# A fused attention and feed-forward kernel: the first batch loaded and ordered anew

## The chip, the core and the metric

The kernel runs on one core of a Trainium2 chip. The core has a matrix engine (TensorE, PE in the profile, with its weight loads listed apart as PEld), a vector engine (VectorE, DVE), a scalar engine (ScalarE, ACT), a general engine (GpSimd, POOL) and a queue engine (SyncE, SP) that only issues transfers. All transfers run on 16 DMA engines. Matrix products are written to PSUM, where this kernel holds eight banks of 2 KB per partition. The metric is the device time of one execution in microseconds, as the median of several runs.

## The reference, cut to what matters

```python
def _attn_ref(q, k, v):                     # (8, 12, 448, 64) each, float32
    scores = (1.0 / np.sqrt(64)) * np.matmul(q, k.transpose(0, 1, 3, 2))
    attn = np.maximum(scores, 0.0) ** 2 / 448
    return np.matmul(attn, v)

x = attn_out.transpose(0, 2, 1, 3).reshape(3584, 768)   # batch*seq, heads*dim
h = x @ w_in                                # w_in (768, 2048)
r = np.maximum(h, 0.0)
out = (r * r) @ w_out                       # w_out (2048, 768)
```

There is no softmax: the scores are cut at zero, squared and multiplied by v. So keys can be added up in any order, and every step after the scores is elementwise or a product.

## The kernel before

**Units and rounds.** The twelve heads of a batch are taken four at a time; such a group is a unit, three to a batch and 24 in all. A unit's 448 keys are cut into seven sets of 64; one set of one unit is a round. For a round the kernel computes scores (L348: 64x64 products, four of them side by side in the array), cuts them at zero out of PSUM into the buffer `rel` (L374 on DVE or L377 on ACT), squares them into `at` or `comb` (L381 on ACT or L383 on POOL) and multiplies by v (L411, again 64x64 products). The result of a unit leaves PSUM as part of `xt` (L431 or L433), the transposed x.

**Getting q and k into shape.** `load_qk` (L241) loads q or k of a unit as float32 (448 KB), `cast_qk` (L266) makes float16 of it in one of three buffers `blk` (L271), and `turn_pe` (L281) turns it: seven 128x128 transposes on PE (L288) into a bank of PSUM and one copy to `qkt` (L291) by DVE or ACT. Later units are turned by a DMA instead. For the first batch, the loads of unit 0 go to buffers `raw`, those of units 1 and 2 into a buffer `early`, which is one of the two large `g` buffers read as float32. The casts of units 1 and 2 are given to POOL alone, that of unit 0 to DVE or ACT. `load_v` (L309) loads v of a unit by two POOL DMAs (L317) that cast to float16 on the way; the quarters of w_in (`load_w1`, L322) and w_out (`load_w2`, L327) are POOL DMAs that cast as well.

**The feed-forward part.** `h_pair` (L488, first batch) and `h_group` (later batches) multiply `xt` with w_in (L472); h is squared by ACT out of PSUM (L461), masked by DVE (L456), and lands in `g`. Output products are L561 for a part of the first batch and L623 later, where a seven-product scheme for 2x2 blocks is used, with sums made by DVE (L602) and of the weights by POOL (L587). Results leave by L545, L547 and L635 and are stored by SP (L510).

**The order of the work.** Every step is added to a list (`Plan.add`) with the engines that may do it, a duration for each, what it depends on, and a due time. `Plan.run` (L71) then walks through a modelled time: whenever an engine is free in the model, `pick` (L152) hands it the waiting step with the earliest due time that is ready and finds free buffers, and the instruction is emitted there and then. The engines run their instructions in exactly this order, so a step that the model takes for late stands behind others even where its data come early. The engine's first free times are given in L230, and until the modelled time `plan.cold` (L231) PE costs are multiplied by 1.6. In the model, transfers pass one after the other at 390 GB/s. A step on PE that is bound to 64x64 products has the mode "tile", others "dense", and the model charges 0.09 or 0.235 us for a change (`SWITCH`).

**The first batch** is written by hand (L752 to L821). PE first runs twelve products on a zeroed buffer (L756). The 448 queries are cut in two parts, 256 and 192 columns. Two rounds make a tile; part 0 has the tiles 0 to 10 and part 1 the tiles 11 to 21 (tile 10 holds one round, as does 21). Tile after tile is scored, with the v products `put` two or three tiles later, and from tile 13 on one h product group of part 0 between (`first_h.popleft()`, L805). The turns of units 1 and 2 stand at tiles 1 to 4, those of unit 3 at tiles 17 and 19 (L778).

Two buffers of two banks each hold scores (`sp`), and four banks (`mm`) serve turns, v products, h and outputs.

Of the kernel before, what the change touches and what calls it, by code (L numbers as in the profile page):

```python
# [41 lines left out]
class Plan:  # L42
# [6 lines left out]
    def __init__(self, pools, busy):  # L49
        self.pools = {name: [(0.0, i, t) for i, t in enumerate(ts)] for name, ts in pools.items()}  # L50
        self.busy = busy
        self.ops: list = []
        self.now = 0.0
# [17 lines left out]
    def run(self):  # L71
# [20 lines left out]
        while done < n_ops:  # L92
# [6 lines left out]
            while again:  # L99
                again = False  # L100
                for eng in ("PE", "ACT", "DVE", "POOL", "SP"):
# [3 lines left out]
                    if got is None:  # L105
                        continue
# [16 lines left out]
                    if size:  # L123
                        dma = max(dma, begin + 1.2) + size / 390e3
                        op.end = dma + 1.0
                    if len(rest) > 1:
                        self.busy["POOL"] = max(self.busy["POOL"], self.busy[eng])
# [23 lines left out]

    def pick(self, eng, now, waiting):  # L152
        for z, (_, _, op) in enumerate(waiting):
            if op.ready > now + 1e-9:
                continue
            for alt in op.alts:
                if alt[0] != eng:
                    continue
                if len(alt) > 5 and self.busy["POOL"] > now + 0.4 and op.due > now:
                    continue  # L160
                need: dict = {}
                for b in op.bufs:
                    if b.tile is None:
                        need[b.pool] = need.get(b.pool, 0) + 1
                if all(sum(x[0] <= now + 1e-9 for x in self.pools[p]) >= k
                       for p, k in need.items()):
                    return z, alt
        return None
# [3 lines left out]
def kernel(  # L172
# [57 lines left out]
    plan = Plan(pools, {"PE": 5.8, "ACT": 2.6, "DVE": 1.2, "POOL": 1.4, "SP": 0.7})  # L230
    plan.cold = 32.0  # L231
# [9 lines left out]
    def load_qk(n, w, after=0.0, gate=False):  # L241
        b, u = divmod(n, NU)
        if n in (1, 2):
            buf, z = early, 2 * n - 2 + (w == "k")
        else:
            buf, z = Buf("raw"), None

        def tile_of():
            if z is None:
                return buf.tile  # L250
            return buf.tile[:, 4 * z:4 * z + 4].rearrange("p f s -> p (f s)").bitcast(
                FP32).rearrange("p (f x) -> p f x", f=2)
# [12 lines left out]

    def cast_qk(n, w, raw, names=("POOL",)):  # L266
# [10 lines left out]
        return plan.add([alts[x] for x in names], [load], [buf, blk]), blk  # L277
# [3 lines left out]
    def turn_pe(n, w, cast, at=None):  # L281
        op, blk = cast
        ps, to = Buf("mm"), Buf("qkt")

        def flip():
            flat = ps.tile.bitcast(FP16)
            for t in range(TJ):
                nc.tensor.transpose(flat[:, t * P:(t + 1) * P], blk.tile[:, t, :], ident)  # L288
# [11 lines left out]
    def turn_dma(n, w, cast):  # L300
        op, blk = cast
# [7 lines left out]
    def load_v(n, after=0.0):  # L309
# [9 lines left out]
        vst[n] = plan.add([("POOL", 1.25, 1.25, emit, QK)], bufs=[buf], after=after), buf  # L319

    def load_w1(i, after):
        return plan.add([("POOL", 0.85, 0.85, lambda: nc.gpsimd.dma_start(  # L322
            out=w1[i], in_=moe_w_in[:, 512 * i:512 * (i + 1)].rearrange(
                "(m p) f -> p m f", p=P)), WQ)], after=after)

    def load_w2(hf, i, after):
# [3 lines left out]
                "(f p) d -> p f d", p=P)), WQ)], after=after)  # L330
# [177 lines left out]
    def store(op, places, cols, osb):  # L508
        def emit(i, b, t):
            return lambda: nc.sync.dma_start(  # L510
# [3 lines left out]
        for i, (b, t) in enumerate(places):  # L514
            plan.add([("SP", 0.56, 3.0, emit(i, b, t))], [op], [osb], due=plan.now + 8.0)
# [167 lines left out]

    fifo: deque = deque()
# [72 lines left out]

    early = Buf("g")
    raws, casts = {}, {}
    for n in range(NU):  # L760
        for w in "kq":
            raws[n, w] = load_qk(n, w)
    for n in range(NU):
        for w in "kq":
            casts[n, w] = cast_qk(n, w, raws[n, w], ("POOL",) if n else ("DVE", "ACT"))
    for n, after in enumerate((1.4, 7.7, 10.0)):
        load_v(n, after)
    w1_ops = [load_w1(0, 12.0), load_w1(1, 13.5)]
    for w in "kq":
        raws[3, w] = load_qk(3, w, 14.5, True)  # L770
    w1_ops += [load_w1(2, 15.0), load_w1(3, 16.0)]
# [6 lines left out]
    turns = {1: (1, "k"), 2: (1, "q"), 3: (2, "k"), 4: (2, "q"), NA + 6: (3, "k"), NA + 8: (3, "q")}  # L778
# [3 lines left out]
    def put(i):  # L782
        part, rs = tiles[i]
        for n, t in rs:
            ats[n, t] = held.pop((part, n, t))
            av(n, [t], PARTS[part])

    for i, (part, rs) in enumerate(tiles):
# [3 lines left out]
        op = scores(rs, [sp], cols, True, 7.6 + 1.25 * i)  # L792
# [7 lines left out]
        if 2 <= i < NA + 2:  # L800
            put(i - 2)
        if i >= NA + 3:
            put(i - 3)
        if i > NA + 1:
            first_h.popleft()[1]()  # L805
        if i == NA:
            for w_ in "kq":
                casts[3, w_] = cast_qk(3, w_, raws[3, w_])
                raws[4, w_] = load_qk(4, w_, 24.0, True)
            load_v(3, 26.0)  # L810
            w2_ops = [[load_w2(hf, z, 29.0 + 6.0 * hf + z) for z in range(2)] for hf in range(2)]
            for w_ in "kq":
                raws[5, w_] = load_qk(5, w_, 35.0, True)
            load_v(4, 36.0)
# [3 lines left out]
    for i in range(len(tiles) - 3, len(tiles)):  # L818
        put(i)
        first_h.popleft()[1]()  # L820
# [37 lines left out]
    for j in sorted(j for j in pushes if j >= NB):  # L858
        push_dense(pushes[j])
    run_some(1e9)  # L860
# [31 lines left out]
```

## Time and profile before

| | us |
|---|---|
| median of 14 runs (lowest, highest) | 398.06 (396.26, 399.56) |
| the profiled execution | 397.69 |
| its span, first to last instruction | 395.9 |
| PE busy in the span | 377.5 (95%) |
| ACT / DVE / POOL busy | 268.6 / 264.6 / 222.8 |
| first score product | 12.41 |
| first h product | 29.04 |

Times within the profile count from the span's start. The line number behind an instruction names the line of the kernel before. In an answer in order of time, the columns are start, duration, engine, line, operation, written from read tile, shapes, count, and in square brackets how long the engine stood idle before it and what released it. In a table of windows each row is a stretch of time, then its length, the busy time of each engine with the number of instructions, the granted TensorE clock as a share of full speed, the busy share of the DMA engines, and GB/s. Matrix products are pipelined and their ends are modelled, so the busy time of PE is no measure of its pace; the distance of the starts is.

### The profile page before, as it was taken

Reading aid. Unit: us, or ns where it says so; the run is one execution under the profiler, and the core shown is the slowest. Engines: PE = TensorE matmul, PEld = TensorE weight load, DVE = VectorE, ACT = ScalarE, POOL = GpSimd, SP = SyncE. Lnnn points to the kernel's source line nnn. Section 1 sums busy time; section 2 is a strip of 40 time slices with the busy share of each in tenths; the row PEclk is TensorE's granted clock in tenths of the full one; section 3 lists DMA queues with packets and bytes.
Section 4 is the critical chain, followed back from the end, with each engine's and each line's share of the span. In section 5 each row is a group of like instructions: output and inputs, shape, how many; then the busy total and the mean of one; then the engine's idle time right before and its main releaser. Section 6 shows DMA issues by size and latency. Waiting matters only on the chain.

```text
span 395.9 us, 8280 instructions
## 1 busy us (share of the span) xinstructions
PE 377.5 (95%) x3264; PEld 199.4 (50%) x3264; DVE 264.6 (67%) x364; ACT 268.6 (68%) x392; POOL 222.8 (56%) x194
## 2 busy tenths in 40 slices
PE   6689999999989999999999999999999999999994
PEld 2466675544445444544455544544554445555562
DVE  1477578367796678776897666865797567455931
ACT  3796799999766688588676677487767776244121
POOL 3999578999948558765555663575452344000100
PEclk9689999999999999999999999999999999999999
DMA  8899999986588776596387685574173002210153
GB/s 270 133 240 244 280 205 285 145 202 141 106 164 175 186 159 93 154 185 114 74 207 171 143 196 117 152 175 89 34 112 80 2 0 55 58 30 0 42 119 80
DMA packets 69670, 53.62 MB, mean 135 GB/s; under 512 B 36864, under 2 KB 69632, under 8 KB 69632
## 3 DMA queue, kind: packets, MB, share of 16 engines
q1 hardware_dynamic: 55152, 40.84, 41.7%
q0 software_dynamic: 14208, 11.80, 20.7%
q8 instruction: 25, 0.41, 0.4%
q10 hardware_dynamic: 272, 0.46, 0.3%
q14 instruction: 13, 0.11, 0.1%
HBM read 45.61 MB, written 11.01 MB: 143 GB/s over the span
## 4 chain that ended last, share of the span: by engine, by line
PE 81%; DVE 7%; ACT 3%; issue 3%; POOL 2%; DMA 2%; SPq 0%; DVEq 0%; POOLq 0%; ACTq 0%
PE mm L472 35%; PE mm L623 26%; PE sp L348 9%; PE mm L411 7%; DVE comb L602 3%; PE mm L561 3%; DVE rel L374 2%; DMA g<-in_q_dram 2%; ACT rel L377 1%; PE mm L288 1%; DVE g L456 1%; POOL at L383 1%; POOL blk L271 1%; POOL wt L587 1%; ACT comb L381 1%
## 5 line engine op out<-in xcount | busy, mean ns | idle before, releaser
L472 PE MATMUL mm<-xt,w 128*128 128x448 f16 (+2 forms) x864 | 157.3, 332 | 0.3 <-DVE g L456 0.3
L383 POOL TENSOR_TENSOR at<-rel 128x896 f16<-128x896 f32 (+1 forms) x60 | 102.6, 1710 | 81.8 <-DVE rel L374 72.1
L374 DVE TENSOR_SCALAR rel<-sp 128x896 f32<-128x896 f32 (+2 forms) x88 | 94.1, 1073 | 36.3 <-PE sp L348 28.9
L472 PEld LDWEIGHTS <-w 128*128 128x128 f16 x864 | 79.1, 98 | 70.7 <-issue 14.0
L456 DVE SCALAR_TENSOR_TENSOR g<-mm,g 128x448 f16<-128x448 f32 (+2 forms) x128 | 79.2, 620 | 49.3 <-ACT g L461 48.9
L461 ACT ACTIVATE g<-mm 128x448 f16<-128x448 f32 (+2 forms) x128 | 68.8, 540 | 45.8 <-PE mm L472 44.2
L381 ACT ACTIVATE at<-rel 128x896 f16<-128x896 f32 (+2 forms) x98 | 91.1, 940 | 8.9 <-DVE rel L374 5.3
L377 ACT ACTIVATE rel<-sp 128x896 f32<-128x896 f32 (+2 forms) x81 | 74.3, 918 | 11.2 <-PE sp L348 10.8
L623 PEld LDWEIGHTS <-comb 128*128 128x128 f16 x416 | 38.9, 98 | 35.8 <-DVE comb L602 6.5
L348 PE MATMUL sp<-qkt,qkt 64*64 64x448 f16 (+2 forms) x756 | 51.6, 349 | 5.2 <-DVE rel L374 2.5
L271 POOL CAST blk<-raw 128x896 f16<-128x896 f32 x42 | 39.9, 957 | 26.1 <-issue 9.4
L545 ACT ACTIVATE part<-mm 128x384 f32<-128x384 f32 x48 | 23.4, 488 | 41.3 <-PE mm L623 39.3
L635 DVE SCALAR_TENSOR_TENSOR part<-mm,part 128x384 f32<-128x384 f32 x52 | 28.3, 551 | 20.6 <-ACT part L545 12.6
L623 PE MATMUL mm<-wt,comb 128*128 128x384 f16 x208 | 37.2, 327 | 2.9 <-DVE comb L602 2.9
L411 PE MATMUL mm<-at,vs 64*64 64x448 f16 (+1 forms) x672 | 37.3, 339 | 0.4 <-POOL at L383 0.4
L623 PE MATMUL mm<-w,comb 128*128 128x384 f16 x208 | 36.9, 327 | 0.4 <-DVE part L547 0.3
L623 PEld LDWEIGHTS <-g 128*128 128x128 f16 x264 | 24.9, 98 | 20.1 <-issue 4.3
L348 PEld LDWEIGHTS <-qkt 64*64 64x64 f16 x756 | 16.7, 108 | 31.5 <-issue 31.1
L623 PE MATMUL mm<-w,g 128*128 128x384 f16 x176 | 31.1, 326 | 0.0
L411 PEld LDWEIGHTS <-vs 64*64 64x64 f16 x756 | 22.9, 108 | 14.6 <-issue 4.6
L317 POOL DMA_DIRECT2D vs<-in_v_dram x48 | 30.1, 633 | 0.1
L527 POOL COPY rest<-g 128x1024 f16<-128x1024 f16 x8 | 10.3, 1287 | 28.9 <-DVE g L456 28.9
(44 smaller groups left out, 219.0 us busy)
## 6 DMA issues: line engine op xcount, KB each, us to landing
out_dram<-part SPq DMA_DIRECT2D x112, 96.0 KB, 2.2
raw<-in_k_dram SPq DMA_DIRECT2D x22, 448.0 KB, 4.3
raw<-in_q_dram SPq DMA_DIRECT2D x21, 448.0 KB, 4.9
vs<-in_v_dram POOLq DMA_DIRECT2D x48, 112.0 KB, 3.2
w<-in_moe_w_in_dram POOLq DMA_DIRECT2D x4, 768.0 KB, 12.7
w<-in_moe_w_out_dram POOLq DMA_DIRECT2D x4, 768.0 KB, 19.0
g<-in_k_dram SPq DMA_DIRECT2D x2, 448.0 KB, 6.7
g<-in_q_dram SPq DMA_DIRECT2D x2, 448.0 KB, 7.7
```

The lines of the kernel that those rows point to most:

```text
L271: return lambda: fn(blk.tile.rearrange("p t (f d) -> p f t d", f=2), tile_of().rearrange("p f (t d) -> p f t d", d=D))
L317: nc.gpsimd.dma_start(out=buf.tile[64 * r:64 * r + 64], in_=src[:, u, hs])
L348: nc.tensor.matmul(sp[64 * c:64 * c + 64, e, c0:c0 + w].rearrange("p (t c) -> p t c", c=TP), lhsT=kT[r, t, 64 * e:64 * e + 64], rhs=qT[r, ...
L374: dve(n, lambda: nc.vector.tensor_scalar(out=rel(), in0=sp.tile[:, :, 0:width], scalar1=0.0, scalar2=SK, op0=ALU.max, op1=ALU.mult)),
L377: act(n, lambda: nc.scalar.activation(out=rel(), in_=sp.tile[:, :, 0:width], func=AF.Relu, scale=SK))],
L381: act(n, lambda: nc.scalar.activation(out=dst(), in_=rel(), func=AF.Square)),
L383: lambda: nc.gpsimd.tensor_mul(dst(), rel(), rel()))],
L411: nc.tensor.matmul(banks[f].tile[64 * e:64 * e + 64, c0:c0 + w], lhsT=vs[r, e ^ c, t * D:(t + 1) * D], rhs=a[r, e, :], start=(t == 0), sto ...
L456: nc.vector.scalar_tensor_tensor(out=dst, in0=src, scalar=0.0, in1=dst, op0=ALU.is_gt, op1=ALU.mult)
L461: nc.scalar.activation(out=dst, in_=src, func=AF.Square)
L472: nc.tensor.matmul(bank.tile[:, c0:c0 + w], lhsT=w1[f // 4][:, m, f % 4 * P:(f % 4 + 1) * P], rhs=xts[b].tile[:, m, cols], start=(m == 0), ...
L623: nc.tensor.matmul(buf.tile[:, 0:HALF], lhsT=lhs()[:, j, :], rhs=w[:, j, :], start=(first and j == 0), stop=(j == NH - 1), skip_group_chec ...
```

## The change

In place of load and cast, q and k of units 1 and 2 now come by GpSimd DMAs that cast to float16 on the way (`load_early`), straight into the early buffer. There is no `blk` and no cast step for them; their turn is fourteen transposes of 128x64 in place of seven of 128x128. The model's first free time of ACT is 0.7 in place of 2.6, with a step without instruction that holds ACT in the model for 1.3 us after the load of q of unit 0; that of PE is 5.0 in place of 5.8, and `plan.cold` is 5.0 in place of 32.

The POOL queue at the start gets due times: k and q of unit 1, v of unit 0, k and q of unit 2, v of unit 1, the first quarter of w_in, v of unit 2, the other three quarters. A rule in `pick` keeps no more than eight of these in flight in the model. Loads of unit 3 move from 14.5 to 20.0.

Wherever PE finds nothing in the model before 45 us and more than one `mm` bank is free, a product of the zeroed buffer with 256 columns is emitted, and the model moves PE on by 0.11 us (`fill`); the mode of PE in the model stays as it was.

Part 1 of the first batch is ordered anew: from tile 13 to 21 only scores with two h groups behind each second tile, the v products of units 0 and 1 together after tile 19, then the turns of unit 3, one h group, the v products of unit 2, and the remaining h groups in a row.

POOL no longer takes a late square where ACT would be done with it sooner, and stores of the last products may be issued by ACT as well as by SP.

```diff
     def run(self):
...
                     got = self.pick(eng, now, waiting)
                     if got is None:
+                        if eng == "PE" and now < self.fill_until:
+                            self.fill(now)
+                            heapq.heappush(events, self.busy[eng])
                         continue
...
                         op.end = dma + 1.0
+                        if eng == "POOL":
+                            self.sent += [op.end] * (2 if size == 458752 and took > 1.0 else 1)
...
+    def fill(self, now):
+        free = [x for x in self.pools["mm"] if x[0] <= now + 1e-9]
+        if len(free) > 1:
+            slot = min(free)
+            self.filler(slot[2])
+            self.pools["mm"].remove(slot)
+            self.pools["mm"].append((now + 0.2, slot[1], slot[2]))
+        self.busy["PE"] = now + 0.11
...
+                if eng == "POOL" and len(op.alts) > 1 and op.due < now and (
+                        max(self.busy["ACT"], now) + 1.1 < now + alt[2]):
+                    continue
+                if len(alt) == 5 and eng == "POOL" and sum(x > now for x in self.sent) > 7:
+                    continue
...
-    plan = Plan(pools, {"PE": 5.8, "ACT": 2.6, "DVE": 1.2, "POOL": 1.4, "SP": 0.7})
-    plan.cold = 32.0
+    plan = Plan(pools, {"PE": 5.0, "ACT": 0.7, "DVE": 1.2, "POOL": 1.4, "SP": 0.7})
+    plan.cold = 5.0
...
+    def load_early(n, w, after, due):
+        z = 2 * n - 2 + (w == "q")
+        def view():
+            return early.tile[:, 2 * z:2 * z + 2]
+        src = (q if w == "q" else k)[0, 4 * n:4 * n + 4].rearrange(
+            "(f e) (p t) d -> (e p) f (t d)", e=2, t=TJ)
+        op = plan.add([("POOL", 0.7, 0.7, lambda: nc.gpsimd.dma_start(out=view(), in_=src), QK)],
+                      [], [early], after=after, due=due)
+        return op, early, lambda t: [
+            (slice(64 * f, 64 * f + 64), view()[:, f, t * D:(t + 1) * D]) for f in range(2)]
...
             for t in range(TJ):
-                nc.tensor.transpose(flat[:, t * P:(t + 1) * P], blk.tile[:, t, :], ident)
+                for r, src in view(t):
+                    nc.tensor.transpose(flat[r, t * P:(t + 1) * P], src, ident)
...
+            ways = [("SP", 0.56, 3.0, emit(nc.sync, i, b, t))]
+            if ending and len(fifo) < 7:
+                ways.append(("ACT", 0.56, 3.0, emit(nc.scalar, i, b, t)))
+            plan.add(ways, [op], [osb], due=plan.now + 8.0)
...
+    plan.fill_until = 45.0
+    plan.filler = lambda bank: nc.tensor.matmul(
+        bank[:, 0:256], lhsT=idle[:, 0:P], rhs=idle[:, 0:256], start=True, stop=True)
...
-    for n in range(NU):
-        for w in "kq":
-            raws[n, w] = load_qk(n, w)
-    for n in range(NU):
-        for w in "kq":
-            casts[n, w] = cast_qk(n, w, raws[n, w], ("POOL",) if n else ("DVE", "ACT"))
-    for n, after in enumerate((1.4, 7.7, 10.0)):
-        load_v(n, after)
-    w1_ops = [load_w1(0, 12.0), load_w1(1, 13.5)]
     for w in "kq":
-        raws[3, w] = load_qk(3, w, 14.5, True)
-    w1_ops += [load_w1(2, 15.0), load_w1(3, 16.0)]
+        raws[0, w] = load_qk(0, w)
+    plan.add([("ACT", 1.3, 1.3, lambda: None)], [raws[0, "q"][0]], due=2.0)
+    for w in "kq":
+        casts[0, w] = cast_qk(0, w, raws[0, w], ("DVE", "ACT"))
+    for w in "kq":
+        casts[1, w] = load_early(1, w, 1.4, 1.0)
+    load_v(0, 1.4, 1.1)
+    for w in "kq":
+        casts[2, w] = load_early(2, w, 1.4, 1.2)
+    load_v(1, 1.4, 1.3)
+    w1_ops = [load_w1(0, 1.4, 1.4)]
+    load_v(2, 1.4, 1.5)
+    w1_ops += [load_w1(i, 8.0, 1.6) for i in range(1, 4)]
+    for w in "kq":
+        raws[3, w] = load_qk(3, w, 20.0, True)
...
+    for i in range(NA):
+        tile(i, 7.6 + 1.1 * i)
+        if i >= 2:
+            put(0, tiles[i - 2][1])
         if i in turns:
             n, w_ = turns[i]
             turn_pe(n, w_, casts[n, w_])
...
+    for i in range(NA + 2, 2 * NA):
+        tile(i)
+        if (i - NA) % 2:
+            some_h(2)
+        if i == NA + 8:
+            put(1, rounds[0:2 * TJ])
+            some_h(1)
+    for w_ in "kq":
+        turn_pe(3, w_, casts[3, w_])
+    some_h(1)
+    put(1, rounds[2 * TJ:])
+    some_h(len(first_h))
     push_dense(0)
```

## The prediction

> **What bounds the kernel now.** I read the page's slices first, then the chain that ended last, then the first 45 us in order of time, since the change is at home there.
>
> ```profile
> PE   6689999999989999999999999999999999999994
> PEclk9689999999999999999999999999999999999999
> ```
>
> PE is full from the fourth slice (30 us) to the last. What the change can win is in the first three slices, where PE has gaps and the granted clock is down, plus what it saves of PE's own time in the first batch and at the end. From about 66 us the chain is nearly all PE, so microseconds won before then should arrive at the end. The chain up to the first scores, and the same stretch in order of time:
>
> ```profile
> 1.77 7.25 DMA g<-in_q_dram
> ...
> 9.07 1.38 POOL blk L271
> ...
> 10.49 0.94 PE mm L288 x7
> 11.45 0.91 ACT qkt L291
> 12.41 0.64 PE sp L348 x7
> ```
>
> ```profile
> 1.20 5.30 PE L756 MATMUL mm<-part 128*128 128x512 f16 x12 [1.20 <-DVE part L753]
> ...
> 5.11 0.94 ACT L271 CAST blk<-raw 128x896 f16<-128x896 f32 x1 [2.57 <-DMA raw<-in_k_dram]
> ...
> 6.90 0.93 POOL L271 CAST blk<-g 128x896 f16<-128x896 f32 x1 [4.08 <-DMA g<-in_k_dram]
> ...
> 8.49 0.62 DVE L291 COPY qkt<-mm 128x896 f16<-128x896 f16 x1 [7.34 <-PE mm L288]
> 9.03 0.61 DVE L271 CAST blk<-raw 128x896 f16<-128x896 f32 x1
> 9.07 1.37 POOL L271 CAST blk<-g 128x896 f16<-128x896 f32 x1 [1.24 <-DMA g<-in_q_dram]
> ```
>
> The only two float32 tiles in `raw` here are k and q of unit 0. q was issued at 0.75 and landed 4.6 us later (the issue rows), at 5.35; DVE casts it at 9.03, because its queue has the copy of unit 1's k in front, which waits for POOL's cast of a late load. The first scores, at 12.41, are those of unit 1, which hang on the fourth transfer. So some 4 us at the start are an order fault. It follows from the code: the model has ACT free only at 2.6, so it takes this load for later than those that SP issues from 0.7.
>
> The second fault is the clock, here by windows:
>
> ```profile
> 10.00:12.00 2.00, 0.93 (x7) 0.79 (x8) 0.00 (x0) 0.55 (x1) 2.00 (x4) 0.50 0.45 139
> 12.00:14.00 2.00, 1.59 (x18) 1.20 (x18) 0.05 (x1) 1.26 (x2) 2.00 (x4) 0.50 0.87 117
> 14.00:16.00 2.00, 2.00 (x28) 1.36 (x26) 1.42 (x3) 1.90 (x3) 2.00 (x3) 0.50 0.72 107
> 16.00:18.00 2.00, 1.39 (x21) 0.80 (x20) 2.00 (x3) 1.84 (x3) 1.15 (x4) 0.82 0.87 101
> ```
>
> Half the clock from 10 to about 17 us (and 0.54 to 0.61 again from 20 to 24). It costs where PE holds others up: the four turns after 12.98 open a hole of 2.18 us between the first two `rel` steps (13.10 and 15.28). After that the elementwise engines set the pace: nine `rel` steps from 15.28 to 23.21, 0.99 us each, with ACT alternating 1.02 (rel) and 1.06 (square) without a gap.
>
> **First scores.** The loads of k and q of unit 0 share the 16 engines with the same three queues as before, so I keep 5.1 and 5.35. ACT casts k by 6.05, DVE q by 6.0. But PE is in its zero products until 6.50 (they stand 0.43 us apart, half pace, where the model thinks PE free at 5.0). Turn of k 6.5 to 7.1; then the model's gap before q's turn is filled with a few zero products (0.11 each, so about 0.5); turn of q to about 8.2, ACT's copy 0.91 and 0.2 of hand-over: scores at about **9.35**, 3.1 earlier. Bounds: 8.5 with no zero product and DVE's 0.62 copy; 10.4 if a dozen run at half pace.
>
> **Part 0 (tiles 0 to 10).** Removed: four POOL casts (0.93 + 1.37 + 0.95 + 0.96 = 4.2 us of POOL); four SP issues. Added on POOL: four q/k issues. No row shows one; a half of v (128 rows) took 0.61, a quarter of w_in (768 rows) 0.86; with 256 rows I take 0.70 each, 2.8 together (2.4 to 3.4). All POOL issues of the start are then 2.8 + 3.7 (v) + 3.4 (w_in) = 9.9 us, from 1.44 to about 12, all ahead of the first square that POOL could take (about 11). Nothing waits behind them but those squares, and ACT covers one or two at 1.06 each. The first `rel` falls at 9.9; at the old pace of 0.99 the tenth is at 18.8, and I add 0.5 because the four `qkt` copies (0.62 on DVE, 2.5 together) now fall among the `rel` steps and not into the hole: 19.3 against 23.21, **3.9 gained** (2.9 if half the hole stays, 5.0 if the pace improves). The new turns are unseen: fourteen products of 128 columns at the 0.08 of the warm turn (0.56 / 7) are 1.1 against 0.56, at half pace 1.9; PE has room here, so I put them at nothing; without that cover they cost 2.2.
>
> A rule that speaks against the change: the Trainium skill, "SBUF — State Buffer", section "SBUF: two separate sides", says that a DVE operation in its two-port mode, such as a float32 `tensor_copy` within SBUF, locks GpSimd out so that it cannot write descriptors for its transfers; the page tells to use the SP or ACT queue instead. The trace has something like such a lock on another operation: POOL's cast at 9.07 runs beside DVE's cast at 9.03 and takes 1.37 where the others take 0.93 to 0.96, 0.43 lost once. The one DVE cast left in the new start (0.61) falls among POOL's issues. By the row it delays one issue by at most 0.6, and the loads behind it have that to spare; by the page, whose example stretches a 620 ns transfer to 3100, 2.5 us could be lost, and q of unit 1 would come at 10 instead of 7.5, still ahead of its tile. I charge nothing, 2.5 at the outer end.
>
> **Loads.** The bytes from memory are the same: 0.459 MB for q, k or v of a unit, 1.573 MB for a quarter of w_in. In the profile the last quarter landed at 39.5 (issue 23.5, 16.0 to landing); by then 10 q/k loads, three v and all of w_in, 12.3 MB, had come in 37.5 us, 327 GB/s. In the new order 8 q/k, three v and w_in are 11.3 MB, so about 36.7 for the last quarter, 31.9 for the third, and, counted the same way, 19.5 for v of unit 2, wanted at about 19.5. Shares with the loads of units 4 and 5 can push the last two quarters 1 to 2 us. I charge **0.3**.
>
> **Part 1.** Before, a dense group of six stands between v products:
>
> ```profile
> 29.99 0.83 PE L472 MATMUL mm<-xt,w 128*128 128x256 f16 x6
> 30.75 0.28 PE L411 MATMUL mm<-at,vs 64*64 64x192 f16 x4
> 30.96 0.83 PE L472 MATMUL mm<-xt,w 128*128 128x256 f16 x6
> ```
>
> 0.97 from group to group; six products of 256 columns at 0.107 are 0.64, four of v about 0.08, which leaves 0.25 for changing modes back and forth. Before, twelve single groups and one run of four make 13 dense stretches; now four pairs, two singles and the last six make 7. Six changes fewer are 1.5 us. The Trainium skill, "TensorEngine Tiling (Array Packing)", section "Key Properties", says that a change of tiling mode drains the engine. That bears on the zero products too: `fill` leaves the model's mode alone, so each one put between two 64x64 products costs 0.11 in the model but by the row 0.11 + 0.25 on the chip. In part 0 PE's gaps hide it; in part 1 they don't. Counted by the row two lone ones take 0.5 back, so **1.0 gained** (-1.0 to 1.5). The point at which twelfth and thirteenth h group meet, before at 45.4 with two rounds and two turns of later units done (about 2.4 us), would then come at 38.1: later than the 36.7 of the last quarter, so the loads stay hidden by 1.4.
>
> **The end.** SP issues the last stores without pause, 0.55 to 0.60 each, and the last of four queued ones at 392.55, while their data were ready at 391.52. ACT, idle there, takes one of each pair: **0.6 gained** (0 to 0.9).
>
> **Sum.** 3.9 + 1.0 + 0.6 - 0.3 = 5.2. Against the profiled execution's own 397.69 that is 392.5; it lies 0.37 below the median of 398.06, so **392.9**. The order of everything later is found anew by the same model, with holes of 2 to 5 us in PE's work such as that at 107 to 114 (sums and `rel` on the chain) that may close or open: 1.5 either way.
>
> **Rivals.**
>
> 1. *Zero products eat PE time (slower).* Place: PE's queue from 25 to 45 us, where PE is full. Each lone one costs 0.36 and the plan knows of 0.11. For: the rule is blind to modes and to PE's real lag. Against: it needs two free banks of four, and scores or h are mostly waiting there. It decides at the gain without their cost, (5.2 + 0.5) / 0.36, some 16 lone ones; at 23, 8.3 us, the time is about **400.7**. 18%.
> 2. *Late transfers.* GpSimd's one queue runs in order, so everything behind v of unit 1 shifts if its transfers run slower than 327 GB/s (291 while two quarters of w_in landed 5.4 us apart). Then the last quarters come 3 us later than PE wants them: **395.5**. 18%.
> 3. *The shift is absorbed.* ACT is 9.97 of 10 us busy from 50 to 60, 9.84 in the next ten; if that stretch, POOL's weight sums behind w_out (fixed at 60 us or later) or a new hole set the time, little is left: **397.9**. 7%.
> 4. *More than forecast*, the hole gone and holes later closed: **388.8**. 7%.
>
> **Numbers.** The forecast, 50%, lies within 390 to 394.8 by its own bounds. The runs of this kernel spread by 0.4% to each side of the median, so a comparison tells about 0.2% from nothing, 0.8 us. Faster by more: the forecast, the second, the fourth and one in a hundred of the third, 76%; within: the rest of the third, 6%; slower: the first, 18%. The range leaves out about one in ten at each end: 389.2 to 399.8.
>
> **What would show it.** First scores between 8.5 and 10.4; the granted clock at 1.00 from 7 us on; tenth `rel` of 1024 elements by 20; no cast into `blk` from `g`; last w_in quarter landed before 38; the first thirteen h groups done by about 39; the first output product (L561, 65.6 before) at about 61. It is wrong if zero products stand between 64x64 products after 25 us in numbers, if PE waits for w_in, or if the 61 isn't kept to the end.

## The result and the profile after

The changed kernel takes **393.29 us** (median of 10 runs, 391.91 to 393.86), beside 398.01 for the kernel before in the same comparison. The ratio, formed over all runs and not from the two medians, is 0.9875, with an interval of 0.9857 to 0.9893. The profiled execution took 393.57 us, with a span of 391.8. Line numbers are now those of the kernel after; its helpers stand some 30 lines lower than before.

The slices of the page, for the tensor engine's busy tenths and its clock:

```profile
PE   8999999999799999999999999999999999999995
PEclk9999999999899999999999999999999999999999
```

The three thin slices at the start (6, 6, 8) are nearly full now, at full clock. But the eleventh slice (98 to 108 us), which was a 9 before, is a 7, and the clock falls in it too. The gain of the start and this new hole are most of the story.

The start in order of time:

```profile
5.39 1.38 DVE L300 CAST blk<-raw 128x896 f16<-128x896 f32 x2 [4.25 <-DMA raw<-in_q_dram]
...
6.29 0.56 PE L319 MATMUL mm<-ident,blk 128*128 128x128 f16 x7
...
7.93 0.58 PE L319 MATMUL mm<-ident,g 128*64 128x128 f16 x14
...
8.98 0.63 PE L379 MATMUL sp<-qkt,qkt 64*64 64x256 f16 x16
```

Unit 0 is now first: DVE takes both casts as the load lands, and the scores start at 8.98 in place of 12.41. The clock by windows, two of those in the prediction and two of the new hole:

```profile
10.00:12.00 2.00, 2.00 (x37) 1.12 (x33) 1.64 (x2) 2.00 (x3) 1.20 (x2) 1.00 1.27 203
...
16.00:18.00 2.00, 2.00 (x38) 1.02 (x33) 1.10 (x2) 2.00 (x3) 0.03 (x1) 1.00 1.24 191
...
100.00:104.00 4.00, 2.32 (x18) 0.96 (x17) 1.45 (x2) 2.75 (x6) 4.00 (x6) 1.00 0.62 100
104.00:108.00 4.00, 3.31 (x31) 1.70 (x31) 3.99 (x5) 3.24 (x5) 2.48 (x2) 0.66 1.03 174
```

The third value from the end is the granted clock: 1.00 from 6.3 us on to the hole; in the first two of these windows it was 0.50 and 0.82 before. From 100 to 104 PE works 2.32 of 4 us, while POOL is busy without a break; then the clock is down. That stretch in order of time:

```profile
94.88 3.11 POOL L621 TENSOR_TENSOR wt<-wt,w 128x1536 f16<-128x1536 f16 x1
...
97.92 1.26 POOL L348 DMA_DIRECT2D vs<-in_v_dram  x2
...
99.15 0.96 POOL L300 CAST blk<-raw 128x896 f16<-128x896 f32 x1
...
100.05 1.71 POOL L414 TENSOR_TENSOR at<-rel 128x896 f16<-128x896 f32 x1
...
101.79 0.92 ACT L408 ACTIVATE rel<-sp 128x896 f32<-128x896 f32 x1 [1.25 <-POOL at L414]
...
102.76 0.38 PE L379 MATMUL sp<-qkt,qkt 64*64 64x448 f16 x4 [0.97 <-ACT rel L408]
...
104.69 2.31 PE L442 MATMUL mm<-at,vs 64*64 64x448 f16 x27 [1.40 <-DVE g L487]
```

Read upward: PE waits for a `rel` of ACT, ACT waits for a square of POOL (it frees the buffer), and that square stands on POOL behind a weight sum, two v issues and a cast, back to back since 94.88. The squaring of h, which ACT has in its queue behind this `rel` and a square, comes late as well (103.44), so DVE's mask (`g`) does, and PE waits another 1.40 for it. Then 27 v products take 2.31, most of them at the lower clock (from 105.25); with the old part 1 and a full clock the whole group of 28 takes 1.49.

To say how far one kernel is ahead of another I count the columns of all matrix products but turns and zero products (those of 64x64 products at a quarter, since four run side by side), and compare the times at which equal shares are done. The lead over the kernel before, in us of the traces:

| kernel | at 67 us | at 103 | at 123 | at 196 | whole span |
|---|---|---|---|---|---|
| the change | 5.8 | 4.3 | 1.7 | 3.2 | 4.1 |
| without zero products (two profiles) | 6.5; 4.6 | 5.0; -0.9 | 2.8; 0.7 | 4.3; 2.4 | 5.1; 2.8 |
| part 1 in old order | 5.1 | 5.1 | 7.1 | 8.6 | 8.8 |
| q and k as before | 2.8 | 2.2 | 4.2 | 5.7 | 6.4 |
| late squares to ACT | 5.8 | 4.3 | 4.1 | 5.6 | 6.5 |
| weight sums open to DVE | 5.9 | 4.7 | 6.4 | 8.1 | 8.7 |

The times at the head are those of the kernel before. Of the two values in the second row the second is that of the kernel that also opens the weight sums to DVE, which is the same program up to 83 us. So the first batch won 5.8, of which 4.1 were lost between 67 and 123; 1.5 came back by 196, and 1.0 was added at the very end. The hole at 100 isn't all of the 4.1: some 1.5 were gone before it, most of them between 80 and 90 us of the change, where ACT is busy 10.00 of 10 us and PE only 9.23. The hole itself takes some 4 us, and part of that shows as regained by 123 because the kernel before then has its own hole.

### The profile page after: what moved, and what is told of

Its sections match the earlier page's. It is cut to its first block, busy times and chain, and to the rows that moved or that the text cites. A ratio compares the mean times of both kernels' runs of the same rounds, so it can differ in the third digit from the quotient of the medians.

```text
span 391.8 us, 8414 instructions
## 1 busy us (share of the span) xinstructions
PE 381.7 (97%) x3344; PEld 200.7 (51%) x3344; DVE 256.0 (65%) x362; ACT 278.9 (71%) x409; POOL 194.9 (50%) x179
## 4 chain that ended last, share of the span: by engine, by line
PE 79%; POOL 6%; ACT 5%; issue 4%; DVE 3%; DMA 1%; SPq 0%; DVEq 0%; POOLq 0%; ACTq 0%
PE mm L503 31%; PE mm L657 29%; PE sp L379 8%; PE mm L442 7%; POOL wt L621 3%; ACT at L412 2%; ACT rel L408 2%; POOL w L621 1%; DMA raw<-in_q_dram 1%; PE mm L794 1%; PE mm L791 1%; DVE rel L405 1%; DVE comb L636 1%; PE mm L319 1%; POOL at L414 1%
## 5 line engine op out<-in xcount | busy, mean ns | idle before, releaser
L414 POOL TENSOR_TENSOR at<-rel 128x896 f16<-128x896 f32 (+1 forms) x47 | 78.1, 1665 | 77.7 <-DVE rel L405 70.9
L405 DVE TENSOR_SCALAR rel<-sp 128x896 f32<-128x896 f32 (+3 forms) x85 | 91.8, 1087 | 35.1 <-PE sp L379 26.1
L412 ACT ACTIVATE at<-rel 128x896 f16<-128x896 f32 (+2 forms) x111 | 103.3, 943 | 3.8 <-PE mm L442 1.1
L408 ACT ACTIVATE rel<-sp 128x896 f32<-128x896 f32 (+2 forms) x84 | 76.4, 913 | 12.8 <-PE sp L379 10.2
L379 PE MATMUL sp<-qkt,qkt 64*64 64x448 f16 (+2 forms) x756 | 50.3, 339 | 2.2 <-ACT rel L408 1.8
L579 ACT ACTIVATE part<-mm 128x384 f32<-128x384 f32 x46 | 22.5, 489 | 38.3 <-PE mm L657 38.1
L442 PE MATMUL mm<-at,vs 64*64 64x448 f16 (+1 forms) x672 | 35.1, 342 | 1.4 <-DVE g L487 1.4
L379 PEld LDWEIGHTS <-qkt 64*64 64x64 f16 x756 | 15.5, 105 | 29.1 <-issue 27.9
L442 PEld LDWEIGHTS <-vs 64*64 64x64 f16 x756 | 20.8, 107 | 15.4 <-issue 5.1
## 6 DMA issues: line engine op xcount, KB each, us to landing
w<-in_moe_w_out_dram POOLq DMA_DIRECT2D x4, 768.0 KB, 18.2
```

Source lines behind the costliest of these rows:

```text
L379: nc.tensor.matmul(sp[64 * c:64 * c + 64, e, c0:c0 + w].rearrange("p (t c) -> p t c", c=TP), lhsT=kT[r, t, 64 * e:64 * e + 64], rhs=qT[r, ...
L405: dve(n, lambda: nc.vector.tensor_scalar(out=rel(), in0=sp.tile[:, :, 0:width], scalar1=0.0, scalar2=SK, op0=ALU.max, op1=ALU.mult)),
L408: act(n, lambda: nc.scalar.activation(out=rel(), in_=sp.tile[:, :, 0:width], func=AF.Relu, scale=SK))],
L412: act(n, lambda: nc.scalar.activation(out=dst(), in_=rel(), func=AF.Square)),
L414: lambda: nc.gpsimd.tensor_mul(dst(), rel(), rel()))],
L442: nc.tensor.matmul(banks[f].tile[64 * e:64 * e + 64, c0:c0 + w], lhsT=vs[r, e ^ c, t * D:(t + 1) * D], rhs=a[r, e, :], start=(t == 0), sto ...
```

## The experiments

Each ratio is to runs of the kernel before taken beside the experiment; their medians lie between 397.21 and 397.79 (398.01 beside the change). So two experiments are better compared by their ratios (0.001 is 0.4 us) than by their medians.

**Zero products.** Are they what keeps the clock up and carries the gain?

```diff
-    plan.fill_until = 45.0
+    plan.fill_until = 0.0
```

> The changed kernel without its 52 zero products in the first 25 us. Theory (the clock is a good part of the gain): the granted clock falls to half within part 0 and again shortly before 24 us, the turns and scores take double the time there; first scores 0.4 earlier (about 8.6), but the thirteenth h group 1.5 later (39.8 against 38.3), the time about 394.5. Rival (PE has room in part 0, the elementwise engines set the pace at any clock): thirteenth h group within 0.5 of 38.3, time 393.0.

Measured: 391.78 us (391.28 to 393.65), ratio 0.9865, 0.9833 to 0.9897. Without them the kernel is no slower, so they don't carry the gain. The thirteenth h group comes at 37.55 in place of 38.30, earlier than theory or rival had it, though the clock is at half from 18.2 to 21.6. What that half costs depends on where it falls; see the run with the same start further down.

**The order alone.** The kernel before, with ACT free at 0.7 in the model and the step that holds it, and nothing else:

```diff
-    plan = Plan(pools, {"PE": 5.8, "ACT": 2.6, "DVE": 1.2, "POOL": 1.4, "SP": 0.7})
+    plan = Plan(pools, {"PE": 5.8, "ACT": 0.7, "DVE": 1.2, "POOL": 1.4, "SP": 0.7})
...
+    plan.add([("ACT", 1.3, 1.3, lambda: None)], [raws[0, "q"][0]], due=2.0)
```

> The kernel before with only the model's first free time of ACT set to 0.7 and the step without instruction behind the load of q of unit 0. Theory (the order fault at the start is the largest single part): first scores at about 9.0 to 9.5 in place of 12.41, thirteenth h group about 42.5 in place of 45.37, first output product about 62.5, and of these 3 us about half at the end: 396.3. Rival (the float32 loads and POOL casts of units 1 and 2 hold the next tiles, so that an earlier start only waits): first scores as early, but thirteenth h group at 45 or later, 397.8.

Measured: 401.02 us (400.17 to 401.85), ratio 1.0088, 1.0059 to 1.0118: slower, which no theory had. The scores start at 8.73 and the first h product at 27.01 (29.04 before). Then, in order of time:

```profile
33.79 0.83 PE L472 MATMUL mm<-xt,w 128*128 128x256 f16 x6 [3.47 <-DMA w<-in_moe_w_in_dram]
...
45.56 0.89 POOL L327 DMA_DIRECT2D w<-in_moe_w_out_dram  x1 [4.04 <-DMA w<-in_moe_w_in_dram]
...
47.44 0.56 PE L288 MATMUL mm<-ident,blk 128*128 128x128 f16 x7 [1.99 <-POOL blk L271]
```

PE waits 3.47 us for a quarter of w_in; POOL stands 4.04 before an issue until a quarter of w_in has landed; its cast comes late, and PE waits again. The thirteenth h group is at 49.81 (45.37 before). The cause stands on POOL, in order of time:

```profile
11.44 1.89 POOL L383 TENSOR_TENSOR comb<-rel 128x1024 f16<-128x1024 f32 x1
...
15.40 1.91 POOL L383 TENSOR_TENSOR comb<-rel 128x1024 f16<-128x1024 f32 x1
...
17.24 0.89 POOL L322 DMA_DIRECT2D w<-in_moe_w_in_dram  x1
```

With the earlier scores there are squares for POOL to take, and it takes them ahead of the w_in issues: the first leaves at 17.24 (14.47 before), and the second quarter lands at 33.75 (29.13 before, in time for this start too). So the early start alone was worth nothing here because it pushed the loads of w_in back.

**Part 1 in its old order.** All of the change but the new part 1:

```diff
     for i in range(NA + 2, 2 * NA):
         tile(i)
-        if (i - NA) % 2:
-            some_h(2)
+        if i >= NA + 3:
+            put(1, tiles[i - 3][1])
+        some_h(1)
+        if i == NA + 6:
+            turn_pe(3, "k", casts[3, "k"])
         if i == NA + 8:
-            put(1, rounds[0:2 * TJ])
-            some_h(1)
-    for w_ in "kq":
-        turn_pe(3, w_, casts[3, w_])
-    some_h(1)
-    put(1, rounds[2 * TJ:])
-    some_h(len(first_h))
+            turn_pe(3, "q", casts[3, "q"])
+    for i in range(2 * NA - 3, 2 * NA):
+        put(1, tiles[i][1])
+        some_h(1)
```

> The changed kernel with part 1 ordered as before (one h group and the v products of one tile behind each tile, turns of unit 3 at tiles 17 and 19). Theory (six changes of mode at 0.25 are saved by the new order): thirteenth h group about 39.8 in place of 38.3, time about 394.0. Rival (the changes hide behind waits for squares): 38.3 within 0.4, 393.3. A third: the new order saves more than the changes, because v products no longer wait for squares in PE's queue: 41 or later, 395.

Measured: 388.95 us (388.59 to 389.63), ratio 0.9787, 0.9766 to 0.9808: faster than the change by 3.5 us by the ratios (4.3 by the medians), which nothing expected had. The thirteenth h group stands at 39.78, as theory had it, but other work is done by then: at 67 us this kernel is only 0.7 behind the change. So the new part 1 won at most that. But this kernel has no hole at 100, and gains where the other loses: POOL has weight sums and casts there as in the change, but no square from 91 to 113 us. PE changes between 64x64 products and the others 30 times from the first to the thirteenth h group before, 12 times in the change, and 16 times here (24 in the order-only kernel): the planner joins h groups by itself, whatever order the hand gives. The edit changes one thing more: the planner finds room for only 26 zero products in place of 52.

**q and k as before.** All of the change, but q and k of units 1 and 2 loaded by SP as float32 and cast by POOL:

```diff
     def load_early(n, w, after, due):
+        z = 2 * n - 2 + (w == "k")
...
+        op = plan.add([("SP", 0.5, 0.5, lambda: nc.sync.dma_start(out=raw(), in_=src), QK)],
+                      [], [early])
+        return cast_qk(n, w, (op, early, raw))
```

> The changed kernel with q and k of units 1 and 2 loaded as float32 by SP and cast by POOL, as before; all else is the changed kernel's. Theory (the order at the start and the clock carry part 0, the casting transfers only free 4.2 us of POOL): first scores at 9.0, tenth rel of 1024 elements about 1 later than 20.1, thirteenth h group about 39.2, time 393.9. Rival (the casting transfers are the heart: POOL's casts stand among the v and w_in issues and delay both): thirteenth h group 41 or later, time 395.5 or more.

Measured: 391.65 us (391.37 to 391.7), ratio 0.9853, 0.9831 to 0.9876. At 67 us its lead is 2.8 in place of 5.8, so the casting transfers, with the order that the planner finds around them, are worth 3.0 there, about half of what the first batch won. The tenth `rel` comes at 21.99 (20.13 in the change), the thirteenth h group at 39.74: nearer to the theory than to the rival, but the theory had given these transfers too little. This kernel too has no hole at 100, and POOL no square between 84 and 115. It ends 0.9 ahead of the change by the ratios (1.6 by the medians).

So the place at 100 us decides more than the parts of the change. The next runs take away what I hold for its cause, a square that comes late on POOL.

**Late squares to ACT.** Rounds 53 to 62, those of the hole, may not be squared by POOL:

```diff
-    def square(op, sp, width, pool="at"):
+    def square(op, sp, width, pool="at", act_only=False):
...
-             lambda: nc.gpsimd.tensor_mul(dst(), rel(), rel()))],
+             lambda: nc.gpsimd.tensor_mul(dst(), rel(), rel()))][:1 if act_only else 2],
...
-            second, at = square(op, sp, S)
+            second, at = square(op, sp, S, act_only=53 <= TJ * n + t <= 62)
```

> The changed kernel with the squares of ten rounds of batch 2 (those due at about 86 to 107 us) given to ACT alone. Theory (the hole at 101 to 109 comes from two squares of 1.7 us that stand on POOL behind weight sums, casts and v issues: ACT's next rel step waits for the buffer, PE waits for ACT, and the clock falls to half): no idle time of PE over 1 us there, clock 1.00 throughout, first h group of batch 2 at about 120.5 in place of 124.5, time about 389.5. Rival (ACT is full there, so the squares' 0.95 each only move the wait; or the weight sums themselves are late): first h group of batch 2 at 123.5 or later, time 392.5 or more.

Measured: 390.92 us (390.74 to 391.21), ratio 0.9837, 0.9805 to 0.9868. The clock stays at 1.00 from 6.1 us to the last product, and the lead at 123 us is 4.1 in place of 1.7. The theory is half right: the first h product of batch 2 comes at 122.13 (124.53 in the change), but not at the expected 120.5, since ACT, now full, leaves PE two gaps of 0.9 near 98 and 102.

**The same edit in the kernel before**, whose hole at 107 to 114 the prediction named:

> The kernel before with the same squares given to ACT alone; in it four stand on POOL between 87 and 107 us and the hole is at 107 to 114. Theory (same cause as in the changed kernel): first h group of batch 2 at about 124 in place of 126.3, time about 395.7. Rival (the hole of the kernel before is the sums of DVE, which have nothing to do with squares): 126 and 397.5 or more.

Measured: 395.23 us (394.8 to 396.32), ratio 0.9945, 0.9926 to 0.9963. Its hole is gone, and the first h product of batch 2 comes at 123.86, as the theory had it. The kernel before, in order of time:

```profile
106.79 2.16 POOL L383 TENSOR_TENSOR at<-rel 128x896 f16<-128x896 f32 x1
...
107.34 2.16 DVE L602 TENSOR_TENSOR comb<-g,g 128x1024 f16<-128x1024 f16 x1
...
110.16 1.47 PE L623 MATMUL mm<-wt,comb 128*128 128x384 f16 x8 [1.21 <-DVE comb L602]
```

and with the square on ACT:

```profile
107.84 0.68 DVE L602 TENSOR_TENSOR comb<-g,g 128x1024 f16<-128x1024 f16 x1
...
108.40 2.76 PE L623 MATMUL mm<-wt,comb 128*128 128x384 f16 x16
```

Here it is not the square that PE waits for. DVE's sum of two tiles, 0.68 when alone, took 2.16: it ended 0.55 after the square did, as if it had only then begun. PE waited for it. This is no single case. The fourteen profiles hold 182 such sums of 128x1024 that took longer than 0.72; all but one, of 0.75, ended 0.54 to 0.56 us after a square, cast or copy of POOL.

**Weight sums open to DVE.** All of the change, and DVE may take the sums of w_out that POOL had alone:

```diff
                 plan.add([("POOL", 3.06, 3.1,
                            lambda r=slice(4 * z, 4 * z + 4), args=args:
-                           nc.gpsimd.tensor_sub(*args(r)))],
+                           nc.gpsimd.tensor_sub(*args(r))),
+                          ("DVE", 0.95, 1.03,
+                           lambda r=slice(4 * z, 4 * z + 4), args=args:
+                           nc.vector.tensor_sub(*args(r)), 0, True)],
```

> The changed kernel with the eight weight sums (3.1 us each on POOL) allowed on DVE too. Theory (POOL's backlog makes the squares late): DVE takes several, POOL is done with its row of work well before 98, no hole at 101 to 109, time about 389.5. Rival (DVE, with g, rel and the output sums, is no less needed there; each sum on it also blocks POOL): a hole elsewhere between 60 and 110, time 392 to 396.

Measured: 389.17 us (388.68 to 391.17), ratio 0.9806, 0.9759 to 0.9853. DVE takes seven of the eight sums and POOL is no longer 3.11 us behind. In the window of the old hole PE is full, at full clock:

```profile
100.00:105.00 5.00, 5.00 (x55) 2.68 (x53) 4.02 (x7) 4.54 (x7) 4.76 (x4) 1.00 0.19 47
```

The lead of 5.9 at 67 us is 6.4 at 123 and 8.7 at the end. The change has the same first batch (5.8 at 67) and ends at 4.1: so the hole, and not the first batch, was what the change lacked.

**The last stores.** All of the change, but SP alone issues the last stores:

```diff
-    ending = True
```

> The changed kernel with all stores on SP. Theory (ACT's stores shorten the tail by 1.0: the last product is 3.1 earlier than before, the end of the span 4.1): last product at about 387.5 as with them, span 392.8, time 394.3. Rival (the tail is shorter for another reason): span within 0.3 of 391.8.

Measured: 395.13 us (393.52 to 396.55), ratio 0.9943, 0.9924 to 0.9961. From the start of the last product to the end of the span it is 5.06 us, against 4.29 in the change: 0.8 from the stores. The medians lie 1.8 apart (2.7 by the ratios), and the rest isn't the stores': PE, DVE, ACT and POOL run the same instructions in the same order, and the trace loses 1.0 at 115 us, where DVE has three instructions in the 4 us from 112 to 116 in which the change has four. So two programs that differ only in who issues the last stores can differ there. Why nearly all runs of this one are slower than those of the change, and not only some, stays open.

**Four combinations** of the edits shown above. First the kernel before with the weight sums open to DVE, to see whether the first batch's gain is the same with that hole treated on both sides:

> The kernel before with the weight sums open to the vector engine, so that the general engine's late squares can no longer hold up the tensor engine at 107 to 114 us. Theory (the change wins 5.7 to 6.5 us in the first batch and about 1 at the end, and all of it reaches the end once no late square stands in the way): this kernel ends about 6.7 us behind the changed kernel with the same edit (389.2), near 395.5 to 396, and its first h product of batch 2 starts near 126 less its hole of about 2, 124. Rival (the first batch's gain is eaten by the full engines after it, whatever becomes of the late squares): it ends near 391 to 392, within 3 us of the other.

Measured: 397.51 us (396.78 to 399.0), ratio 0.9996, 0.998 to 1.0012. The rival is out, since the two kernels stand 8.3 apart (7.6 by the ratios). The theory's figure is missed as well: the edit buys the kernel before nothing. In order of time (the profiled run took 398.73, 1.2 more than the median):

```profile
66.50 5.38 DVE L590 TENSOR_TENSOR wt<-w,wt 128x1536 f16<-128x1536 f16 x2
...
66.87 1.71 POOL L383 TENSOR_TENSOR at<-rel 128x896 f16<-128x896 f32 x1
...
68.50 2.56 POOL L271 CAST blk<-raw 128x896 f16<-128x896 f32 x2
...
72.93 0.38 PE L348 MATMUL sp<-qkt,qkt 64*64 64x448 f16 x4 [1.70 <-DVE rel L374]
```

Two sums that take 0.95 each alone took 3.77 and 1.68 beside POOL's square and casts. DVE's `rel` came late, PE lost some 2 us at 71, and at 110 a sum of DVE was stretched again, to 2.34. What the edit does depends on what POOL runs beside it.

Then the sums on DVE without zero products:

> The change with the weight sums open to the vector engine and without the added zero products. Theory (they cost the tensor engine some 0.7 us net, up to the thirteenth h group): 388.4, thirteenth h group near 37.5, first h product of batch 2 near 119.1. Rival (the order found anew gives it back): 389.2, as with the zero products.

Measured: 393.43 us, with runs from 389.68 to 394.87, ratio 0.9873, 0.9814 to 0.9932. Both expectations are missed by the median, and the profiled run (394.87) is the slowest; the one run of 389.68, with a mean clock of 0.998 in place of 0.987 to 0.991, came near the rival's 389.2. The profiled run shows two things. Up to 83 us its instructions on PE are those of the first experiment, yet from 24 us on it runs 2.0 behind. Two windows of that first experiment:

```profile
18.00:20.00 2.00, 1.80 (x28) 1.28 (x28) 2.00 (x3) 2.00 (x4) 0.00 (x0) 0.56 1.24 207
...
26.00:28.00 2.00, 2.00 (x25) 1.50 (x24) 0.39 (x1) 1.59 (x3) 2.00 (x5) 1.00 1.15 271
```

and of this one:

```profile
18.00:20.00 2.00, 1.30 (x28) 0.76 (x28) 2.00 (x3) 2.00 (x4) 0.00 (x0) 1.00 1.26 210
...
26.00:28.00 2.00, 2.00 (x11) 1.45 (x10) 0.00 (x0) 0.88 (x2) 1.94 (x5) 0.50 1.14 272
```

The half clock came at 18.2 to 21.6 there and at 21.8 to 28.6 here. In the first place PE does its 28 products from 18 to 20 all the same, since DVE and ACT set the pace (2.00 of 2 us busy). The second is twice as long and reaches to where PE is the bound: it does 11 from 26 to 28 where the other does 25. The second thing is a hole at 86 us, in order of time:

```profile
87.15 4.97 POOL L414 TENSOR_TENSOR at<-rel 128x896 f16<-128x896 f32 x3
...
88.89 0.92 ACT L408 ACTIVATE rel<-sp 128x896 f32<-128x896 f32 x1 [4.11 <-POOL at L414]
...
89.86 0.40 PE L379 MATMUL sp<-qkt,qkt 64*64 64x448 f16 x4 [3.10 <-ACT rel L408]
```

It is the chain of the change's hole at another place: POOL, late with casts and v issues, takes three squares in a row; ACT waits for a buffer, and PE for ACT.

Last, the old part 1 with the sums on DVE, with and without zero products:

> The change with part 1 in its old order and the weight sums open to the vector engine. Theory (the new order of part 1 wins about 1.5 us at the thirteenth h group, 38.30 against 39.78, and that arrives once no late square stands behind it): 390.5 to 391, slower than the changed kernel with the same edit (389.2). Rival (the new order of part 1 wins nothing that lasts): 388.5 to 389.

Measured: 390.08 us (389.76 to 390.58), ratio 0.9805, 0.9776 to 0.9834.

> The same, without the added zero products as well. Theory: 390, 0.7 less than with them and 1.5 more than the changed kernel with only the other two edits (388.4). Rival (neither the zero products nor the order of part 1 last to the end): 388.5 to 389.2.

Measured: 388.69 us (388.54 to 388.92), ratio 0.9769, 0.9735 to 0.9803. The first lies between theory and rival, the second is the rival's: with neither the new part 1 nor the zero products the kernel is as fast as any. Three kernels, this one, the one with only the old part 1 (388.95) and the one with only the sums (389.17), are 2.7 to 4.2 us faster than the change by the ratios (about 4 by the medians); the runs don't tell them apart.

## Why the prediction was right, step by step

The total was 392.9 and 393.29 was measured. The sum of 5.2 against the profiled execution was 4.1, and it hides errors that partly cancel: the first batch was put at 4.6 and won 5.8, the end at 0.6 and won 1.0, and 2.7 net went between them, most of it to a hole, where the sum had only 1.5 either way. The start is right in its mechanism; that the total is met so closely is in part luck.

- **First scores, 9.35; measured 8.98.** The order fault was read rightly. DVE, not ACT, took the cast of k, and the 11 zero products before the scores cost less than the 0.5 put: without them the scores start at 8.71.
- **Part 0, 3.9 gained; measured 3.1 at the tenth `rel`** (20.13 against 23.21; 19.3 was forecast). Without zero products it is 19.39, a gain of 3.8. So the step was right but for one clause: that PE's gaps hide the zero products there. They cost 0.7 at that point. The new turns were put at 1.1 us for fourteen products and took 0.58, no more than seven of the old kind; the q and k issues at 2.8 and took 3.15.
- **Part 1, 1.0 gained; of the 5.8 won by 67 us, part 0 leaves 2.7.** The size of a change of modes held: two h groups stand 1.05 apart (28.97 and 30.02) with eight score products between, which leaves 0.25 as before. There are 18 changes fewer, at half of 0.25 some 2.2. Their place was wrong. With the old part 1 there are already 14 fewer, some 1.8 us, and the old order's lead at 67 us is 5.1 to 5.8 in three kernels. The new order by itself is worth at most 0.7. The step "thirteenth h group at 38.1" was met at 38.30.
- **Loads, 0.3 lost, the last quarter at 36.7; measured 33.4,** the third at 26.6 in place of 31.9. Nothing was lost. The 327 GB/s were an average over a start in which w_in was first issued at 14.47; now it is at 6.96. The second rival did not come about; what late loads cost shows in the order-only run, where PE waited 3.47.
- **The rule on DVE and POOL.** The Trainium skill, "SBUF — State Buffer", section "SBUF: two separate sides", was weighed for the start only, and the row was right: v's issue at 5.67 beside DVE's casts took 1.25 for two, as elsewhere. But the same section says that the pair of ports they share is an exclusive lock, taken also by a DVE operation with two inputs in SBUF against a GpSimd operation that reads SBUF. That I didn't apply, and the runs agree with it: 0.68 became 2.16, and 0.95 became 3.77, beside POOL's squares and casts, and 181 of 182 stretched sums ended 0.54 to 0.56 us after a POOL instruction.
- **The first rival, zero products.** 52 were added, all before 25.5 us, ahead of the first h group; the place it named, from 25 to 45 us, stayed free but for three at its very start. What the prediction missed is the other side: their use. With them the thirteenth h group came at 38.24 to 38.39 in each of four profiles; without, at 37.55 and 39.55. They cost 0.7 or save 1.3, by where the clock's low stretch falls.
- **The third rival, a new hole,** had 7% and in part came true: 4.1 us went between 67 and 123, and the change ends 4.1 ahead instead of near 8. Its other branch, ACT without a pause, has a share too: the 1.5 us before the hole. One of the prediction's own signs of being wrong came true with it: the first output product was earlier than forecast (57.59 for 61), and the gain wasn't kept to the end. The prediction named the hole of the kernel before and let it go as "1.5 either way"; the step that failed is that one. That hole could have been followed to its end: a `comb` of 2.16 where its fellows take 0.68, beside a POOL square of 2.16. With the late squares on ACT the lead at 123 us grew by 2.4 in both kernels, with the sums on DVE by 4.7 in the change (in the kernel before, where they met POOL at 66, it fell by 1.2).
- **The end, 0.6; measured 1.0** by the distance from the last product to the end of the span (5.32 to 4.29), of which ACT's stores are 0.8 by the run without them; the other 0.2 is open.

What stays open: why the planner's order leaves POOL late at just these places. The model knows POOL's durations well in the mean, and it knows the lock for DVE's sums: the `True` behind them in `plan.add` makes a sum wait until POOL is free in the model, and holds POOL meanwhile. But that holds in modelled time; on the chip sum and square met all the same. No run here tells how far the two times had drifted apart there. The rule that keeps late squares from POOL and the cap of eight transfers in flight were not tested alone. Nor is it settled how much of the 1.5 us regained by 196 belongs to the change.

## What to carry to other kernels

An order found by a planner shifts as a whole when its start shifts, so a change at the start must be judged with the holes behind it: follow each hole of the profile before to the engine that ends it, and give that engine relief in the same step. Where an early start is won, look at what it lets the issuing engine do first: here squares went ahead of the load issues, and the start was given back at the first late load. And sums of VectorE in SBUF should not stand beside elementwise work of GpSimd (here 0.68 us became up to 2.5); a row whose duration varies threefold is a sign of it.

## What was not expected of the hardware

- A float16 sum of two SBUF tiles on VectorE takes 0.68 us (128x1024) or 0.95 (128x1536) alone, and up to 2.5 and 3.8 while GpSimd squares, casts or copies; the shorter of the two then ends some 0.55 us after a GpSimd instruction, in 181 of 182 cases. GpSimd's square, 1.67 to 1.71 otherwise, went to 2.16 in the same place.
- The clock fell to half at 105.25 for 3.4 us after gaps in the starts of the products of 1.35 and 1.74 us with a few products between. The Trainium skill, "TensorE: Matmul & The Clock Gate", section "Why this matters for your kernels", asks for no gap above some 3 us; here two shorter ones, close together, came before it, and in the run without zero products one of 1.74; yet a gap of 2.07 in another run (at 70.9, the kernel before with the sums on DVE) was followed by none. So the length of a gap alone doesn't decide. Up to the last product, every low stretch in the fourteen profiles lasts 3.41 us or twice that.
- A half clock from 18.2 to 21.6 us cost nothing that shows, one from 21.8 to 28.6 in the same instructions 2.0 us. What a low clock is worth is read from who sets the pace at that moment.
- Fourteen transposes of 128x64 take 0.58 us, seven of 128x128 take 0.56.
